# Reordering the gate/up steps of a two-layer Strassen kernel, and counting VectorE's 16-bit sums as held by GpSimd in its planner

## The chip, the cores and the metric

The kernel runs on one core of one Trainium2 chip. The metric is the device time of one execution in microseconds. The median of the kernel before is 1450.27 us over three runs (1448.57 to 1450.39).

## The reference, cut to what matters

Two kinds of block alternate, each added to its own input, on 2048 tokens of width 1024:

```python
def _A_ref(x, wqkv, wo):            # linear attention, 32 heads of 32
    q, k, v = heads(x @ wqkv)
    phi = lambda t: where(t > 0, t + 1, exp(t)) + 1e-6
    pq, pk = phi(q), phi(k)
    kv, z = einsum("bhsd,bhse->bhde", pk, v), einsum("bhsd->bhd", pk)
    o = einsum("bhqd,bhde->bhqe", pq, kv) / (einsum("bhqd,bhd->bhq", pq, z)[..., None] + 1e-6)
    return unheads(o) @ wo

def _B_ref(x, w_gate, w_up, w_down):   # F = 3584
    return ((x @ w_gate) * (x @ w_up)) @ w_down

x = x + _A_ref(_layernorm(x), A_wqkv, A_wo)
x = x + _B_ref(_layernorm(x), B_w_gate, B_w_up, B_w_down)
x = x + _A_ref(_layernorm(x), A_wqkv, A_wo)
x = x + _B_ref(_layernorm(x), B_w_gate, B_w_up, B_w_down)
```

Both A blocks use the same weights, and both B blocks too. So there are two layers, each an A block followed by a B block.

## The kernel before, in words

**Stages.** Each layer runs its A block as three stages: the key and query projections, the products that build the state ("g", with the normalization of the attention output), and the output projection ("y"). Then comes the B block in two halves of 1024 tokens. Each half is a gate/up stage followed by a down stage. There are so four gate/up stages, named here by layer and half: 1a, 1b, 2a, 2b. In the code their keys are `(False, 0)`, `(False, 1)`, `(True, 0)` and `(True, 1)`, where the first entry says "not the first layer" and the second is the half.

**A gate/up stage.** It has 14 *pairs* (`pair`, L1512). A pair is two *units* A and B, two blocks of 128 columns of w_gate (pairs 0, 2, 4 ...) or of w_up (pairs 1, 3, 5 ...). Each pair multiplies weights by activations with Strassen's seven products, numbered 1 to 7, instead of eight. Those products named in `L2SETS` (L357) use Strassen once more inside themselves: 5 in stage 1a; 5, 4 and 2 in stage 1b; 2, 5, 4 and 1 in the stages of layer 2. A plain product of one unit is four matmuls of 512 columns (L1539). A second-level product is done for both units at once by fourteen matmuls of 256 columns (L1657).

**Steps.** The order of a pair's work is a list of tokens written out by hand in `ORDERS` (L358). `gateup` (L1719) walks through that list once for each pair p and emits the instructions of each token, and every engine runs its own instructions in that order. A token with a prime (') does the step for pair p-1, one with a plus does it for p+1, so pairs overlap. At the end of the stage the primed tokens are emitted once more for the last pair (the *tail*), after the first matmuls of the down stage. The tokens are:

- `P1A`, `P6B` ...: the plain product of that number for unit A or B. TensorE does four matmuls, ScalarE copies the result to SBUF where a later step needs it (L1544), or into another PSUM bank (L1574).
- `51`, `55`, `56`, `57` (and `2n`, `4n`, `1n`): the steps of second-level product 5 (2, 4, 1). Each is two matmuls of 256 columns. Steps n1, n5 and n7 end in ScalarE copies (L1661, L1673); steps n6 and n7 end in a VectorE sum into PSUM (L1664), called a *seed* here.
- `D5A` and so on: the last products of a number into its result bank. For a second-level number A is four matmuls of 256 columns and B two.
- `F2A` and so on: the eviction. VectorE takes the result out of PSUM (L920). In an even pair the value is stored. In an odd pair it must also be multiplied into the value of the pair before (gate times up): VectorE writes one of three buffers (`utmp`) and GpSimd multiplies (L1563). In stage 1a evictions 1 and 4, which add nothing, are done by ScalarE in even pairs and by VectorE alone in odd ones.
- `S24`, `S5`, `S1`: the weight sums for the second level. In layer 1 they are four VectorE sums of 512 elements (`S24`) or of 256 elements (`S5`, `S1`) in 16 bits (all through the helper at L917), stored to DRAM for later; in layer 2, and `S5` in stage 1b, they are a DMA load instead.
- `T0`, `T1`: other work in small pieces (layer norm, saving the residual). In stage 1a they also make the first-level sums of a later unit (`prep_s`, L982: four VectorE sums of 512 elements, from the raw weights of that unit), store them to DRAM, and do the sums for the down weights (`wd_prep`).
- `R`: two loads of unit weights into a ring of five slots (`ring_issue`, L873). In iteration p it loads units 2p+3 and 2p+4 (counted from 0; pair p has units 2p and 2p+1). Every DMA of the kernel goes through the queue of SyncE in order of emission.
- `HA`, `HB`: nothing but, in stage 2a, four loads of the residual after the last pair.

**The planner.** Three kinds of section are not in the order of emission but in one found by a list scheduler (`reorder`, L155): the key/query stage of layer 2 (tag "kq2"), and the g and y stages of layer 1 (tags "g1" and "y1"). It gives each instruction a cost (`_cost`, L46 to L93) and a due time, makes twelve passes (`_pass`, L206) and keeps the order in which TensorE waits least by these costs. The last of the four values that `_cost` returns says whether the instruction needs the SBUF port that VectorE and GpSimd are taken to share: `_pass` starts such an instruction only when the one before it of that kind, on either engine, has ended (`gate`, L246).

Of the kernel before, what the change touches and what calls it, by code (L numbers as in the profile page):

```python
# [49 lines left out]
def _cost(op):  # L50
    seen = _Seen()
    op.fn(seen)
    name, args, kw = seen.calls[0]
    aps = [a for a in list(args) + list(kw.values()) if hasattr(a, "shape") and hasattr(a, "tensor")]

    def free(a):
        return int(np.prod(a.shape[1:]))

    def half(a):
        return a.dtype in (BF16, mybir.dt.float16)  # L60
    n = max(free(a) for a in aps)
    psum = any(a.tensor.name == "ps" for a in aps)
    packed = all(half(a) for a in aps if free(a) > 1)
    k = len(seen.calls)
    if op.eng == "sp":
        size = float(np.prod(aps[0].shape)) * (2 if half(aps[0]) else 4)
        if "transpose" in name:
            return 1240, 1240, size / 200, False
        return 70, 70, size / 300, False
    if op.eng == "pe":  # L70
        cols = free(args[0]) if name == "matmul" else 128
        one = max(cols / 2.4 + 2.5, 25)
        return k * one, (k - 1) * one + cols / 2.4 + 166, 0, False
    if op.eng == "act":
        c = 0.87 * n + 75
        return c, c + 104, 0, False
    if op.eng == "pool":
        c = 0.8 * n + 60 if name == "memset" else (580 if name == "tensor_tensor" else 304) if n < 64 else \
            (2.2 if packed else 2.45) * n if name == "tensor_tensor" else 1.15 * n + 20
        return c, c + 45, 0, n >= 64 and name != "memset"  # L80
    if name in ("bn_stats", "bn_aggr"):
        c = 635 if name == "bn_stats" else 126
    elif name == "tensor_reduce":
        c = 1150
    elif n < 64:
        c = 130 if name != "reciprocal" or n < 16 else 270
    elif name == "tensor_tensor":
        c = n / 1.92 + 68 if packed and not psum else n / 0.96 + 70
    elif name == "tensor_scalar" and not psum:
        c = n / (3.84 if packed else 1.92) + (140 if n > 512 else 70)  # L90
    else:
        c = n / 0.96 + 70
    return c, c + 84, 0, n >= 64 and not psum and name in ("tensor_scalar", "tensor_copy")  # L93


class _Prog:
# [58 lines left out]
    def reorder(self, tags):  # L155
# [6 lines left out]
        for e in _ENGS:  # L162
# [6 lines left out]
            for (_, ga), (_, gb) in zip(runs, runs[1:]):  # L169
                for x in gb:  # L170
                    preds[x].update(ga)
        occ, lat, load, port = zip(*(_cost(o) for o in ops))
        succ = [[] for _ in range(n)]
        for i in range(n):
# [160 lines left out]
def build_kernel(nc, A_x, A_wqkv, A_wo, B_w_gate, B_w_up, B_w_down, out):  # L335
# [20 lines left out]

    L2SETS = {(False, 0): "5", (False, 1): "542", (True, 0): "2541", (True, 1): "2541"}  # L357
    ORDERS = {  # L358
# [4 lines left out]
    }  # L363
    MUL_ENG = "pool"
# [125 lines left out]
    with ExitStack() as es:  # L490
# [13 lines left out]
        def vh(o, n):  # L504
            return ah[:, o // 2: o // 2 + n]
# [17 lines left out]
        T1, T2, T4 = [vh(O_T + i * 4096, 2048).rearrange("p (k s) -> p k s", s=512) for i in range(3)]  # L523
# [1749 lines left out]
def bass_interleave_layers__linear_attn_block__glu_gated_bilinear__prompt_kernel(  # L2273
    nc, A_x, A_wqkv, A_wo, B_x, B_w_gate, B_w_up, B_w_down, out,
):
    build_kernel(nc, A_x, A_wqkv, A_wo, B_w_gate, B_w_up, B_w_down, out)
# [28 lines left out]
```

## Time and profile before

| what | value |
|---|---|
| median of three runs | 1450.27 us |
| the profiled execution: its own time | 1451.07 us |
| the profiled execution: span on the core | 1449.3 us |
| granted TensorE clock | 1.00 |
| TensorE busy | 1426.1 us, 98% |
| VectorE busy | 1211.0 us, 84% |
| ScalarE busy | 618.9 us, 43% |
| GpSimd busy | 440.8 us, 30% |

The stages lie one after another in the span: gate/up 1a from about 240 to 411 us, 1b from 494 to 674 us, 2a from 970 to 1130 us and 2b from 1209 to 1369 us, with the down stages behind each. The key/query stage of layer 2 is at 748 to 846 us.

How to read it: in the views by window a row gives the length of the stretch, then for each engine its busy time and, in brackets, how many instructions lie in it, then the granted clock, the busy share of the DMA engines and the rate. In a timeline a row is the start, the time taken, the engine, the line, the operation, what it writes and reads, and how many neighbours were merged into the row; in square brackets stands the idle time before it and what ended it. Neighbours on VectorE overlap by some 0.1 us at their ends, so four sums in one row take less than four times one. Busy times of TensorE have modelled ends.

### The profile page before, as it was taken

To read this page: it belongs to the slowest core of one execution; us is meant where nothing else is said; L and a number is where in the kernel's file an instruction comes from. 1 tells how busy PE (TensorE), PEld (TensorE's weight loads), DVE (VectorE), ACT (ScalarE), POOL (GpSimd) and SP (SyncE) were. 2 spreads that over 40 slices of the span, in tenths; PEclk is the share of its full clock that TensorE was granted. 3 is DMA by queue.
4 is the path that set the end of the run, shared out by engine and by line. 5 is a ranking of instruction groups with operands and counts; after the bars stand their busy time and mean duration, and the time that the engine had idled before them with its cause. 6 is when DMAs were issued, how large, how long until landed. Compare 5 with 4: busy or idle time off the path is not lost.

```text
span 1449.3 us, 22852 instructions
## 1 busy us (share of the span) xinstructions
PE 1426.1 (98%) x8362; PEld 800.9 (55%) x8417; DVE 1211.0 (84%) x2282; ACT 618.9 (43%) x1292; POOL 440.8 (30%) x436
## 2 busy tenths in 40 slices
PE   9999999999999999999999999999999999999999
PEld 4444444454444555556574444456666677666557
DVE  8988898998968799998899869787877897777697
ACT  4332365444410255542037732566666114666402
POOL 4544631121210034342014447213443201342400
DMA  7446776999899889988782667688998769999667
GB/s 239 102 106 182 163 167 176 285 309 301 286 303 330 282 272 284 282 268 269 272 300 68 187 189 149 166 223 269 287 294 273 269 228 317 298 293 296 232 204 235
DMA packets 367040, 349.91 MB, mean 241 GB/s; under 512 B 107472, under 2 KB 308688, under 8 KB 366928
## 3 DMA queue, kind: packets, MB, share of 16 engines
q1 hardware_dynamic: 366928, 348.45, 79.5%
q8 instruction: 67, 1.10, 0.3%
q14 instruction: 45, 0.37, 0.1%
HBM read 255.72 MB, written 71.57 MB: 226 GB/s over the span
## 4 chain that ended last, share of the span: by engine, by line
PE 87%; DVE 7%; DMA 3%; issue 1%; ACT 1%; SPq 0%; POOL 0%; DVEq 0%; ACTq 0%
PE ps L1539 23%; PE ps L1657 16%; PE ps L1980 13%; PE ps L1097 8%; PE ps L2061 8%; PE ps L1440 8%; PE ps L1332 7%; PE ps L1161 3%; DVE arena L917 3%; DVE arena L920 2%; DMA arena<-in_B_w_gate_dram 1%; DVE ps L1664 1%; DMA arena<-in_A_wqkv_dram 1%; DMA arena<-xn_scratch 1%; PE ps L1355 0%
## 5 line engine op out<-in xcount | busy, mean ns | idle before, releaser
L1539 PE MATMUL ps<-arena 128*128 128x512 f16 x1824 | 453.2, 379 | 4.9 <-DVE arena L920 4.0
L920 DVE SCALAR_TENSOR_TENSOR arena<-ps,arena 128x512 f16<-128x512 f32 (+2 forms) x562 | 372.2, 683 | 70.7 <-PE ps L1980 29.7
L1563 POOL TENSOR_TENSOR arena<-arena 128x512 f16<-128x512 f16 x196 | 225.2, 1170 | 581.5 <-DVE arena L920 579.1
L917 DVE TENSOR_TENSOR arena<-arena 128x512 f16<-128x512 bf16 (+7 forms) x648 | 342.4, 569 | 15.3 <-PE ps L2061 4.9
L1657 PE MATMUL ps<-arena 128*128 128x256 f16 x2296 | 311.9, 273 | 6.3 <-DVE ps L1664 5.6
L1544 ACT ACTIVATE arena<-ps 128x512 f32<-128x512 f32 x308 | 184.3, 598 | 241.9 <-PE ps L1539 186.5
L1657 PEld LDWEIGHTS ps<-arena 128*128 128x128 f16 (+1 forms) x2296 | 214.8, 98 | 123.8 <-DVE ps L1664 27.5
L1539 PEld LDWEIGHTS ps<-arena 128*128 128x128 f16 (+1 forms) x1824 | 175.5, 98 | 150.9 <-DVE arena L920 9.8
L1664 DVE TENSOR_TENSOR ps<-ps,arena 128x256 f32<-128x256 f32 x328 | 141.2, 431 | 81.6 <-ACT ps L1661 34.7
L1980 PE MATMUL ps<-arena 128*128 128x512 f16 (+1 forms) x885 | 194.2, 379 | 1.0 <-POOL arena L1563 0.4
L1661 ACT COPY ps<-ps 128x256 f32<-128x256 f32 x328 | 109.9, 361 | 110.3 <-PE ps L1657 83.5
L1980 PEld LDWEIGHTS ps<-arena 128*128 128x128 f16 x896 | 87.3, 98 | 104.9 <-POOL arena L1563 0.9
L2061 PE MATMUL ps<-arena 128*128 128x256 f16 (+1 forms) x1176 | 129.8, 273 | 0.2
L1097 PE MATMUL ps<-arena 128*128 128x512 bf16 x563 | 125.8, 379 | 1.3 <-DMA arena<-in_A_wqkv_dram 0.5
L2061 PEld LDWEIGHTS ps<-arena 128*128 128x128 f16 x1176 | 114.7, 98 | 15.6 <-ACT ps L2067 1.0
L1332 PE MATMUL ps<-arena 128*128 128x512 bf16 x499 | 114.9, 379 | 2.0 <-DMA arena<-xn_scratch 1.0
L1440 PE MATMUL ps<-arena 128*128 128x512 bf16 x502 | 110.3, 379 | 0.5
L1226 POOL TENSOR_TENSOR arena<-arena 128x1024 f16<-128x1024 f32 x32 | 80.8, 2525 | 85.5 <-DVE arena L1224 82.8
L1120 POOL TENSOR_TENSOR arena<-arena 128x512 f32<-128x512 f32 x60 | 72.6, 1216 | 80.0 <-DVE arena L811 40.7
L1097 PEld LDWEIGHTS ps<-arena 128*128 128x128 f16 x576 | 55.8, 98 | 67.0 <-DMA arena<-in_A_wqkv_dram 1.4
L618 DVE BATCH_NORM_STATS2 arena<-arena 128x6 f32<-128x512 bf16 x128 | 87.8, 688 | 5.6 <-DMA arena<-in_A_x_dram 3.7
L1161 PE MATMUL ps<-arena 128*128 128x512 f16 (+1 forms) x385 | 85.4, 379 | 1.5 <-DVE arena L831 0.6
(69 smaller groups left out, 950.6 us busy)
## 6 DMA issues: line engine op xcount, KB each, us to landing
arena<-s_scratch SPq DMA_DIRECT2D x84, 512.0 KB, 6.3
arena<-d_images SPq DMA_DIRECT2D x36, 896.0 KB, 5.3
arena<-in_B_w_gate_dram SPq DMA_DIRECT2D x56, 512.0 KB, 5.9
arena<-in_B_w_up_dram SPq DMA_DIRECT2D x56, 512.0 KB, 5.5
arena<-t_scratch SPq DMA_DIRECT2D x20, 896.0 KB, 4.9
arena<-p_scratch SPq DMA_DIRECT2D x66, 256.0 KB, 4.6
s_scratch<-arena SPq DMA_DIRECT2D x28, 512.0 KB, 6.4
arena<-p_scratch SPq DMA_DIRECT2D x28, 512.0 KB, 5.7
```

Source lines behind the costliest of these rows:

```text
L917: P.add("dve", lambda e: e.tensor_tensor(out=out, in0=a, in1=b, op=op), rd=rd, wr=wr, prd=prd)
L920: P.add("dve", lambda e: e.scalar_tensor_tensor(out=out, in0=a, scalar=sc, in1=b, op0=ALU.mult, op1=op1), rd=rd, wr=wr, prd=prd)
L1097: P.add("pe", lambda e: [e.matmul(psb(bank), xnT[:, k, i * 128:(i + 1) * 128], w[:, k, h * 512:(h + 1) * 512], start=(k == 0), stop=(k == ...
L1332: return [e.matmul(psb(bank), xr[:, t, j * 128:(j + 1) * 128], pk[:, h, t, :], start=(start and t == ts[0]), stop=(stop and t == ts[-1]), ...
L1440: return [e.matmul(psb(bank), xnT[:, g, i * 128:(i + 1) * 128], wp[:, g, dh * 512:(dh + 1) * 512], start=(dh == 0 and g == 0), stop=(g == ...
L1539: P.add("pe", lambda e: [e.matmul(psb(bank), w[:, k, :], x[:, k, :], start=(start and k == 0), stop=(k == 3), skip_group_check=True) for k ...
L1544: P.add("act", lambda e: e.activation(t, psb(bank), AF.Copy, scale=SG), prd=[bank], wr=r)
L1563: P.add(MUL_ENG, lambda e: e.tensor_tensor(out=hx, in0=ut, in1=hx, op=ALU.mult), rd=ur + hr, wr=hr)
L1657: P.add("pe", lambda e: [e.matmul(psb(bank)[:, 256 * half:256 * half + 256], w[:, k, :], xx[:, k, :], start=(start and k == 0), stop=(k == ...
L1664: P.add("dve", lambda e: e.tensor_tensor(out=psb(bank)[:, 256:512], in0=psb(src)[:, 0:256], in1=c5, op=ALU.add), prd=[src], rd=rc5, pwr=[b ...
L1980: P.add("pe", lambda e: [e.matmul(psb(bank), hv[:, 7 * hf + k, t * 128:(t + 1) * 128], w[:, k, :], start=(q in fresh and hf == 0 and k == ...
L2061: P.add("pe", lambda e: [e.matmul(half(b, h), x[:, k, :], w[:, k, :], start=(bool(start) and k == 0), stop=(k == 6), skip_group_check=True ...
```

## The change

Two things are changed. First, in `_cost` VectorE's `tensor_tensor` on operands that are all 16 bits wide and lie in SBUF now counts as needing the shared port, as `tensor_scalar` and `tensor_copy` did already. Its assumed duration is the same. This is used by the planner alone, so it acts on the order in "kq2", "g1" and "y1". Second, three of the four token lists are replaced (1a, 1b and 2a); that of 2b stays.

```diff
-    return c, c + 84, 0, n >= 64 and not psum and name in ("tensor_scalar", "tensor_copy")
+    return c, c + 84, 0, n >= 64 and not psum and (name in ("tensor_scalar", "tensor_copy") or packed and name == "tensor_tensor")
...
     ORDERS = {
-        (False, 0): "51' P7A' 55' P6B' F1A' T0' 56' HA' D4A' F4A' HB' T1' P7B' D2B' 57' P1A D5A' F2A' D4B' D2A S5 D5B' F2B' D3A' F4B' F3A' F1B' P6A D3B' F3B' R P1B",
-        (False, 1): "P7A' D2B' F1B' HA 57' 41' D5A' 45' F2A' P7B' 46' P1A S5 D5B' S24 D3A' T0' F2B' 47' D4A' F4A' S1' 21 25 P1B D3B' D4B' 26 F3A' R P6A F4B' F3B' HB 27 51 P6B D2A 55 F1A 56 T1'",
-        (True, 0): "P7A' 41' HB' D5A' HA' F2A' 57' P7B' D2B' 45' F1B' 46' D5B' F2B' D3A' S24 47' S1+ 11 D4A' 15 16 D3B' F4A' 17 21 P1A F3A' D4B' 25 26 P1B F4B' P6A F3B' 51 27 P6B D2A S5 F1A 55 56 T0 R T1",
+        (False, 0): "56' P7A' P6B' HB' D5A' D4A' T0' F2A' F4A' 57' P7B' D2B' F1B' T1' P1A D5B' D4B' D2A F2B' F4B' R D3A' F3A' P6A HA' 51 S5 F1A P1B D3B' 55 F3B'",
+        (False, 1): "D2B' F1B' 55' 56' T1' P7A' 57' 41' P7B' 45' S1' 46' D5A' D5B' S5 S24 F2A' F2B' P1A HA 47' D4A' F4A' P1B 25 21 D3A' F3A' P6A T0 D4B' 51 26 HB F4B' D3B' F3B' 27 D2A P6B F1A R",
+        (True, 0): "D2A' 55' F1A' HA' HB' 56' T1' P7A' 41' D5A' F2A' 57' P7B' D2B' 45' F1B' S1+ 46' D5B' F2B' D3A' 47' 11 D4A' 15 16 F4A' D3B' 17 S5 21 P1A 25 F3A' S24+ D4B' 26 F4B' T0 R F3B' P1B P6A 51 27 P6B",
```

Every list holds the same tokens as before apart from their primes and pluses, so the number of instructions of each kind in a stage is the same; only their order on the engines and in SyncE's queue changes.

## The prediction

> **What bounds the kernel now.** I read the page's head first, then the stages by windows (columns as explained above).
>
> ```profile
> PE 1426.1 (98%) x8362; PEld 800.9 (55%) x8417; DVE 1211.0 (84%) x2282; ACT 618.9 (43%) x1292; POOL 440.8 (30%) x436
> ```
> ```profile
> 113.80:183.60 69.80, 69.38 (x371) 33.70 (x378) 58.39 (x82) 19.69 (x33) 36.52 (x15) 1.00 0.72 185
> 183.60:239.50 55.90, 55.64 (x256) 25.25 (x258) 51.13 (x115) 32.68 (x45) 17.17 (x30) 1.00 0.73 175
> 239.50:410.90 171.40, 168.52 (x874) 84.65 (x873) 147.59 (x339) 78.08 (x155) 32.22 (x30) 1.00 0.92 280
> ...
> 494.00:674.30 180.30, 171.50 (x1063) 99.38 (x1063) 162.96 (x339) 88.02 (x210) 69.64 (x72) 1.00 0.88 272
> ...
> 747.90:846.30 98.40, 95.45 (x431) 42.12 (x438) 88.61 (x183) 70.66 (x117) 43.39 (x48) 1.00 0.58 176
> ...
> 969.70:1130.40 160.70, 160.60 (x1108) 104.58 (x1109) 121.66 (x234) 100.58 (x246) 61.63 (x57) 1.00 0.84 264
> ...
> 1208.90:1368.60 159.70, 159.59 (x1105) 104.42 (x1105) 114.81 (x221) 99.65 (x245) 58.43 (x53) 1.00 0.91 281
> ```
>
> TensorE is the bound, and its idle time lies in few places: 8.80 us in stage 1b (180.30 - 171.50), 2.88 in 1a, 2.95 in the key/query stage, 0.10 in 2a, 0.42 and 0.26 in g and y of layer 1. Only these can be won. Stage 1b has fewer matmuls than 2a (1063 against 1108) and takes 19.6 us longer, with VectorE busy for 162.96 us of it. The chain that ended last gives the pace:
>
> ```profile
> 505.82 1.73 PE ps L1539 x8
> ...
> 656.58 1.73 PE ps L1539 x8
> ...
> 850.18 3.45 PE ps L1332 x16
> ...
> 991.76 1.81 PE ps L1657 x16
> ...
> 1117.30 1.82 PE ps L1657 x16
> ```
>
> In 1b the same piece returns every two pairs, six times in 150.76 us: 25.13 us for two. In 2a a piece returns every pair, eleven times in 125.54 us: 11.41. A matmul of 512 columns takes 3.45/16 = 0.216 us, one of 256 takes 1.81/16 = 0.113. A pair of 1b has 32 and 42 of them, one of 2a 24 and 56, so on TensorE alone 1b would need 11.41 + 8 x 0.216 - 14 x 0.113 = 11.56 us a pair, 23.12 for two. Lost are 2.0 us in every two pairs, **14 us** in the stage's seven.
>
> Where they go, a timeline shows. The same sums stand in it twice, four of 256 and four of 512 elements, in two successive iterations:
>
> ```profile
> 581.24 1.01 DVE L917 TENSOR_TENSOR arena<-arena 128x256 f16<-128x256 bf16 x4
> ...
> 583.29 1.88 DVE L920 SCALAR_TENSOR_TENSOR arena<-ps,arena 128x512 f16<-128x512 f32 x3
> ...
> 589.73 2.52 POOL L1563 TENSOR_TENSOR arena<-arena 128x512 f16<-128x512 f16 x2 [1.26 <-DVE arena L920]
> ...
> 590.83 2.51 DVE L917 TENSOR_TENSOR arena<-arena 128x512 f16<-128x512 bf16 x4
> ...
> 594.58 1.04 PE L1539 MATMUL ps<-arena 128*128 128x512 f16 x4 [0.95 <-DVE arena L920]
> 594.61 2.32 POOL L1563 TENSOR_TENSOR arena<-arena 128x512 f16<-128x512 f16 x2 [2.35 <-DVE arena L920]
> ...
> 595.37 2.23 DVE L917 TENSOR_TENSOR arena<-arena 128x256 f16<-128x256 bf16 x4
> ...
> 598.00 0.61 PE L1657 MATMUL ps<-arena 128*128 128x256 f16 x4 [0.79 <-DVE ps L1664]
> ...
> 598.23 0.63 SPq L589 DMA_DIRECT2D arena<-in_B_w_up_dram  x1
> ...
> 604.17 1.55 DVE L917 TENSOR_TENSOR arena<-arena 128x512 f16<-128x512 bf16 x4
> ```
>
> Where GpSimd multiplies, `S24` takes 2.51 instead of 1.55 us and `S1'` 2.23 instead of 1.01; TensorE then waits on VectorE (0.95, 0.79). The excess is 0.96 + 1.22 = 2.18 us in one iteration of two, 15.3 in seven: the size of the loss. Without it VectorE has 162.96 - 15.3 = 147.7 us, 10.5 a pair against TensorE's 11.56.
>
> **Part 1, the list of 1b.** It moves the sums away from the multiplies, if my placing by hand is right. Two durations for it, from the page's groups:
>
> ```profile
> L1664 DVE TENSOR_TENSOR ps<-ps,arena 128x256 f32<-128x256 f32 x328 | 141.2, 431 | 81.6 <-ACT ps L1661 34.7
> ...
> L618 DVE BATCH_NORM_STATS2 arena<-arena 128x6 f32<-128x512 bf16 x128 | 87.8, 688 | 5.6 <-DMA arena<-in_A_x_dram 3.7
> ```
>
> TensorE's positions in the new list (0.216 and 0.113 a matmul, from the start of an iteration): D2B' ends at 0.2, 57' 1.7, 46' 3.2, D5B' 3.9, D4A' 5.4, D3A' 7.6, D4B' 8.7, 26 9.1, D3B' 9.9, 27 10.2, D2A 10.6, the end at 11.6. VectorE's order is F1B' 56' T1' 57' S1' 46' S24 F2A' F2B' 47' F4A' F3A' T0 26 F4B' F3B' 27 F1A. An eviction takes 0.63 in a row of three (1.88/3), a seed 0.34 (0.43 less the 0.1 by which neighbours overlap), a T some 0.7, one `bn_stats`. F1B' runs from 0.4, S1' from 2.7 to 3.7, S24 from 4.0 to 5.6, F2A' and F2B' to 6.9, F4A' to 7.8, F3A' to 8.4, T0 to 9.1, F4B' and F3B' to 10.8, the seed of 27 to 11.2, F1A to 11.8. VectorE keeps up, by some 0.3 us.
>
> Multiplies exist for odd pairs, so in one iteration of two. F1A's runs to about 1.6 of the next iteration and F1B's to 2.8 (2.52/2 = 1.26 each); the other six begin at 6.2, when both sums are over. They run seven to eight us and end near 2 in the iteration after, ahead of S1' again. So S24 is free and S1' touches the end of one multiply. In the old order F1B' and F2A' came before S24, and F2B' and F4A' before S1'. From both sides: all 14 us won, or none. I take a remainder of 0.35 us in each of seven iterations, between the 0.1 us of overlap that I place and the 0.96 that a whole S24 pays now: 14 - 2.5 = **-11.5 us**.
>
> `R` moves to the end, and its weights are needed by the next iteration's S24 at 4.0, so by 15.6. SyncE reaches it behind S24's store (5.6) and, where T0 stores a norm, behind that (9.1). That leaves 6.5 to 10 us. Before, loads issued at 598.23 fed S24 at 604.17, 5.9 us later, without a wait in that row. I cost it at nothing.
>
> **Part 2, the list of 1a.** Two stalls stand out, one view for the wait and one for the load; the third fence is the page's:
>
> ```profile
> 284.19 2.35 DVE L917 TENSOR_TENSOR arena<-arena 128x512 f16<-128x512 bf16 x6 [1.39 <-DMA arena<-in_B_w_gate_dram]
> ...
> 357.45 2.35 DVE L917 TENSOR_TENSOR arena<-arena 128x512 f16<-128x512 bf16 x6 [2.10 <-DMA arena<-in_B_w_gate_dram]
> ```
> ```profile
> 276.38 7.79 DMA arena<-in_B_w_gate_dram
> ...
> 349.15 8.28 DMA arena<-in_B_w_gate_dram
> ```
> ```profile
> arena<-in_B_w_gate_dram SPq DMA_DIRECT2D x56, 512.0 KB, 5.9
> ```
>
> The load waits in SyncE's queue behind the store of S5's sums. In the new list R stands ahead of S5, after D4B' at 7.2, and T1' needs the data after D2B' at 5.2 rather than before it: two to three us more lead, above the 2.10 that was missing. Won: up to 3.5 us (1.39 + 2.10). Against it, T0' now runs ahead of F4A', and T1' ahead of F4B'. With 2.35 us for its six sums and 0.7 for a norm, F4A' of an odd pair ends near 5.0 where P1A wants its bank at 5.2, and F4B' near 9.9 where P1B wants its bank at 10.0. A miss of up to 0.7 in each of seven iterations costs 5 us; I take 2. S5's sums now fall beside F3A's multiply, where VectorE has the lighter next iteration to catch up. Sum **-1.5 us**, bounds -3.5 and +5.
>
> **Part 3, the list of 2a.** Cyclically TensorE's order is the old one but for D4B' and 25 changing places; the list begins elsewhere, so the tail is longer and the first iteration shorter. Its sums are loads, S24 a pair earlier and S5 later. TensorE idles 0.10 us here: **0**, bounds -0.1 and +1, about one step's chain of copies at the start.
>
> **Part 4, the planner.** Neither engine's work changes. In the key/query stage 2.95 us are idle; I take **-0.5**, bounds -3 and +3 (as much again). g and y have 0.7 idle together: 0, to +2, one misplaced product of L1226 (row below).
>
> The rule that speaks against this part is told beside its rows:
>
> ```profile
> L1226 POOL TENSOR_TENSOR arena<-arena 128x1024 f16<-128x1024 f32 x32 | 80.8, 2525 | 85.5 <-DVE arena L1224 82.8 <-DVE arena L640 2.7
> ...
> L1217 DVE TENSOR_TENSOR arena<-arena 128x1024 f32<-128x1024 bf16 x20 | 23.5, 1182 | 0.1
> ...
> L1214 DVE SCALAR_TENSOR_TENSOR arena<-arena 128x1024 f32<-128x1024 bf16 x12 | 16.8, 1401 | 0.0
> ```
>
> The Trainium skill (SBUF — State Buffer, "Who interferes with whom") lets any VectorE instruction with two SBUF inputs contend with a GpSimd instruction that reads SBUF, whatever its width. By that rule the norm's products L1217 and L1214 would be held too while the planner still counts them free; the means here do not show a hold, and the sum by the rule would take the +2 of g and y.
>
> **Sum.** -11.5 - 1.5 + 0 - 0.5 = -13.5 us, made against the profiled execution: 1451.07 (span 1449.3) to 1437.6. The median lies 0.8 lower, 1450.27, so **1436.8 us**.
>
> **The rivals.** *Half of it (1444).* VectorE keeps up in 1b by 0.3 us only, and D2B' needs the seed of 27, which stands behind F4B' and F3B'. An extra piece of norm in T (0.7) or a held S1' then makes TensorE wait 0.4 to 0.7 in most iterations: 14 x 0.5 = 7 back, -6.5. For it: VectorE's 10.5 of 11.56. Against: iterations without multiplies keep up now with the same work.
>
> *The holds stay (1448).* The multiplies follow the evictions wherever these go; if GpSimd runs a multiply or two later than I place it, S1' and S24 fall under it as now, and only the 2.0 of the other parts is won. Against: six of eight evictions now stand behind S24.
>
> *Late weights in 1b (1459, slower).* If SyncE comes to R only in its place, after F1A and D2A at 10.6, S24 has 5.0 us where a load takes 5.9 in the median and 7.79 or 8.28 at worst. VectorE would stand still there and everything queued behind S24 with it, F2A' first, then TensorE. VectorE's slack is 1.06 a pair, so the loss is 13 x (wait - 1.06): with 7.79 it is 13 x (2.79 - 1.06) = 22, less the 13.5 of the sum, so 9 us slower than before. It decides above a wait of 2.1 us, where 13 x 1.04 eats the 13.5. For it: the DMA share of 1b rises from 0.88 to some 0.94 as the stage shortens. Against: the lead above, and 2b, at 0.91 with R last in its list, idles 0.11 us.
>
> *The planner's stages lose (1442):* the bounds above, +5, taken with the rest won.
>
> **Chances.** Forecast 0.55 (its own range 1433 to 1441), half 0.20, planner 0.06, holds stay 0.09, late weights 0.10. About 0.2% (2.9 us) is what a measurement can tell from no change. Faster by more: 0.55 + 0.20 + 0.06, same 0.09, slower 0.10. The range is 1431 to 1448: below, all of 14 + 3.5 + 3 less 1; above, the half (-6.5) with 1a at +2.5 in place of -1.5, some 4 us more.
>
> **What would show it.** Part 1: in 1b's groups the 256- and 512-element sums of L917 fall from means of 489 and 563 ns to about 290 and 420, and two pairs take 23 to 23.5 us. The group rows for that:
>
> ```profile
> L917 DVE TENSOR_TENSOR arena<-arena 128x512 f16<-128x512 bf16 x39 | 20.9, 563 | 0.4
> L917 DVE TENSOR_TENSOR arena<-arena 128x256 f16<-128x256 bf16 x42 | 19.4, 489 | 0.5
> ```
>
> Part 2: no wait for w_gate above 1 us in 1a; against it, waits of L1539 on L920 there. Part 3: 2a within 1 us of 160.7. Part 4: TensorE's idle time in 748 to 846. Wrong would be a gap on VectorE ahead of S24 put down to w_gate or w_up (late weights), or idle TensorE ahead of D2B' put down to L1664 (half).

## The result, and the profile after

The changed kernel takes 1438.74 us (median of four runs, 1438.32 to 1439.24) against 1450.33 us beside it. The ratio is 0.9919, with a 95% interval of 0.9902 to 0.9936: 0.8% faster, 9 to 14 us. The forecast was 1436.8 us, with a range of 1431 to 1448.

The page of the changed kernel, its head and the first groups:

```profile
span 1436.9 us, 22892 instructions
PE 1427.0 (99%) x8417; PEld 804.0 (56%) x8417; DVE 1196.4 (83%) x2282; ACT 618.8 (43%) x1292; POOL 438.7 (31%) x436
...
PE 94%; DVE 2%; ACT 1%; DMA 1%; issue 0%; SPq 0%; POOL 0%; DVEq 0%; ACTq 0%
...
L1539 PE MATMUL ps<-arena 128*128 128x512 f16 x1824 | 449.5, 379 | 0.7 <-ACT ps L1574 0.7
```

The last two of these rows, on the page of the kernel before:

```profile
PE 87%; DVE 7%; DMA 3%; issue 1%; ACT 1%; SPq 0%; POOL 0%; DVEq 0%; ACTq 0%
...
L1539 PE MATMUL ps<-arena 128*128 128x512 f16 x1824 | 453.2, 379 | 4.9 <-DVE arena L920 4.0
```

The span is 12.4 us shorter (1449.3 to 1436.9). VectorE does the same 2282 instructions in 14.6 us less (1211.0 to 1196.4), and of the chain that ended last 94% is now TensorE's instead of 87%. TensorE's wait ahead of L1539 fell from 4.9 to 0.7 us. By stages (from the start of the first matmul to the start of the last one for a gate/up stage; for the others from there to the first matmul of the next):

| stage | before, us | after, us | difference |
|---|---|---|---|
| gate/up 1a | 171.9 | 168.6 | -3.3 |
| gate/up 1b | 175.2 | 167.6 | -7.7 |
| the down stage behind 1b | 78.8 | 78.1 | -0.7 |
| key/query of layer 2 | 93.3 | 92.9 | -0.4 |
| gate/up 2a | 161.4 | 161.0 | -0.3 |
| gate/up 2b (list not changed) | 161.0 | 161.9 | +0.9 |
| all others | 607.7 | 606.8 | -0.9 |

Of the 0.9 of 2b, 0.7 is a wait of TensorE for a load from `p_scratch` at its start. The stage ran from 161.0 to 162.8 us in the kernels below, all with the same 2b list, so it is not counted as an effect of the change.

Stage 1b by window, in the changed kernel:

```profile
490.00:658.00 168.00, 165.99 (x1046) 100.01 (x1045) 148.99 (x338) 86.79 (x210) 65.10 (x69) 1.00 0.96 291
```

In 1b VectorE is busy for 148.99 us instead of 162.96, and TensorE is idle for 2.01 us (168.00 - 165.99) instead of 8.80. The groups of its sums in that window, and the wait that stayed:

```profile
L917 DVE TENSOR_TENSOR arena<-arena 128x512 f16<-128x512 bf16 x40 | 15.7, 419 | 0.5
...
L917 DVE TENSOR_TENSOR arena<-arena 128x256 f16<-128x256 bf16 x42 | 10.8, 285 | 0.5
L655 DVE TENSOR_SCALAR arena<-arena 128x1024 f16<-128x1024 bf16 x8 | 6.2, 775 | 2.0 <-POOL arena L634 2.0
```

The means fell from 563 and 489 ns to 419 and 285. The timeline of 1b shows where the multiplies went, and one iteration that is still late:

```profile
537.25 6.72 POOL L1563 TENSOR_TENSOR arena<-arena 128x512 f16<-128x512 f16 x6 [3.97 <-DVE arena L920]
...
545.63 0.55 DVE L655 TENSOR_SCALAR arena<-arena 128x1024 f16<-128x1024 bf16 x1 [1.00 <-POOL arena L634]
546.09 0.43 DVE L1664 TENSOR_TENSOR ps<-ps,arena 128x256 f32<-128x256 f32 x1
...
546.42 1.01 DVE L917 TENSOR_TENSOR arena<-arena 128x256 f16<-128x256 bf16 x4
...
546.57 0.39 PE L1657 MATMUL ps<-arena 128*128 128x256 f16 x2 [0.37 <-DVE ps L1664]
```

Six multiplies run in one block from 537.25 to 543.97, after both sums of their iteration; the next S1' at 546.42 takes 1.01 us, unheld. Ahead of it VectorE stood still for 1.00 us until GpSimd had finished a small chain for a norm (L634), so the seed at 546.09 came late and TensorE waited 0.37. The pace of 1b in the chain of the changed kernel:

```profile
525.96 1.73 PE ps L1539 x8
537.60 1.73 PE ps L1539 x8
549.96 1.82 PE ps L1539 x8
561.70 1.73 PE ps L1539 x8
574.06 1.83 PE ps L1539 x8
```

An iteration takes 11.64 us (537.60 - 525.96) where nothing waits, and 12.36 where the norm is late (549.96 - 537.60 and 574.06 - 561.70). Two iterations are 23.28 us without such a wait (2 x 11.64) and 24.10 with one (561.70 - 537.60). Before, two iterations took 25.13.

### The profile page after: what moved, and what is told of

Same layout as the page of the kernel before. It is cut to its first block, busy times and chain, and to the rows that moved or that the text cites. A ratio compares the mean times of both kernels' runs of the same rounds, so it can differ in the third digit from the quotient of the medians.

```text
span 1436.9 us, 22892 instructions
## 1 busy us (share of the span) xinstructions
PE 1427.0 (99%) x8417; PEld 804.0 (56%) x8417; DVE 1196.4 (83%) x2282; ACT 618.8 (43%) x1292; POOL 438.7 (31%) x436
## 4 chain that ended last, share of the span: by engine, by line
PE 94%; DVE 2%; ACT 1%; DMA 1%; issue 0%; SPq 0%; POOL 0%; DVEq 0%; ACTq 0%
PE ps L1539 27%; PE ps L1657 17%; PE ps L1980 13%; PE ps L1097 9%; PE ps L1440 8%; PE ps L2061 8%; PE ps L1332 7%; PE ps L1161 4%; DVE arena L920 1%; DMA arena<-xn_scratch 1%; PE ps L1355 1%; PE ps L1383 0%; DMA arena<-p_scratch 0%; ACT arena L652 0%; DVE arena L618 0%
## 5 line engine op out<-in xcount | busy, mean ns | idle before, releaser
L1539 PE MATMUL ps<-arena 128*128 128x512 f16 x1824 | 449.5, 379 | 0.7 <-ACT ps L1574 0.7
L1563 POOL TENSOR_TENSOR arena<-arena 128x512 f16<-128x512 f16 x196 | 223.8, 1163 | 477.4 <-DVE arena L920 475.0
L917 DVE TENSOR_TENSOR arena<-arena 128x512 f16<-128x512 bf16 (+7 forms) x648 | 326.7, 544 | 12.1 <-PE ps L2061 4.9
L1657 PE MATMUL ps<-arena 128*128 128x256 f16 x2296 | 308.2, 273 | 2.7 <-DVE ps L1664 2.0
L1539 PEld LDWEIGHTS ps<-arena 128*128 128x128 f16 (+1 forms) x1824 | 176.4, 98 | 146.3 <-ACT ps L1574 1.2
L1980 PE MATMUL ps<-arena 128*128 128x512 f16 (+1 forms) x896 | 195.2, 379 | 0.0
L1226 POOL TENSOR_TENSOR arena<-arena 128x1024 f16<-128x1024 f32 x32 | 80.5, 2515 | 85.6 <-DVE arena L1224 81.4
L1161 PE MATMUL ps<-arena 128*128 128x512 bf16 (+1 forms) x392 | 85.6, 379 | 0.8 <-ACT ps L1182 0.8
```

The lines of the kernel that those rows point to most:

```text
L917: P.add("dve", lambda e: e.tensor_tensor(out=out, in0=a, in1=b, op=op), rd=rd, wr=wr, prd=prd)
L1161: P.add("pe", lambda e: [e.matmul(psb(bank), l[:, k, :], w[:, k, :], start=(start and k == 0), stop=(k == 3), skip_group_check=True) for k ...
L1539: P.add("pe", lambda e: [e.matmul(psb(bank), w[:, k, :], x[:, k, :], start=(start and k == 0), stop=(k == 3), skip_group_check=True) for k ...
L1563: P.add(MUL_ENG, lambda e: e.tensor_tensor(out=hx, in0=ut, in1=hx, op=ALU.mult), rd=ur + hr, wr=hr)
L1657: P.add("pe", lambda e: [e.matmul(psb(bank)[:, 256 * half:256 * half + 256], w[:, k, :], xx[:, k, :], start=(start and k == 0), stop=(k == ...
L1980: P.add("pe", lambda e: [e.matmul(psb(bank), hv[:, 7 * hf + k, t * 128:(t + 1) * 128], w[:, k, :], start=(q in fresh and hf == 0 and k == ...
```

## The experiments

### Each part by itself

Four kernels carry one edit each: the planner's line, or one of the three lists as the change has it.

```diff
# e1_cost: the kernel before, and
+    return c, c + 84, 0, n >= 64 and not psum and (name in ("tensor_scalar", "tensor_copy") or packed and name == "tensor_tensor")
# e2_1b: the kernel before, with the new list of (False, 1)
# e3_1a: the kernel before, with the new list of (False, 0)
# e4_2a: the kernel before, with the new list of (True, 0)
```

> The kernel before with the planner's cost line alone (16-bit VectorE sums counted as needing the shared port); the four token lists stay old. Theory: the stages that the planner orders idle little, so this part is worth -0.5 us or less (1449.8), with the key/query stage of layer 2 some 0.3 us shorter. Rival, the planner carries a good share of the gain (the sums of the key/query stage are no longer held): -2 to -4 us. Other rival, it loses: +1 to +3.

> The kernel before with the new token list of stage 1b alone. Theory: this list is the larger part; -7.7 us in the stage and -0.7 in the down stage behind it (TensorE no longer waits for a multiply there), so 1442. Rival, 1b gains only together with 1a (its first weights and residuals come from 1a's queue order): -4 or less.

> The kernel before with the new token list of stage 1a alone. Theory: the two waits for w_gate go, -3.3 us (1447.0), and nothing else moves. Rival, what 1a wins is lost again in the down stage behind it or in 1b: within 1 us of before.

> The kernel before with the new token list of stage 2a alone. Theory: TensorE idled 0.1 us in this stage, so nothing to win: within 0.7 us of 1450.3. Rival, the longer tail and later loads cost: +1 to +2.

| kernel | ratio to before, 95% interval | its own stage, us |
|---|---|---|
| planner's line | 0.9994 (0.9985 to 1.0003) | key/query 93.3 to 92.8 |
| list of 1b | 0.9945 (0.9933 to 0.9958) | 1b 175.2 to 167.2, down stage behind it 78.8 to 78.1 |
| list of 1a | 0.9974 (0.9965 to 0.9983) | 1a 171.9 to 168.7 |
| list of 2a | 0.9999 (0.9990 to 1.0008) | 2a 161.4 to 161.1 |

The parts add up: the four ratios multiply to 0.9912, and all together measured 0.9919. Two thirds of the gain is 1b, nearly all the rest 1a. For the planner's line and for 2a no effect can be told from none in the time. Of the two kinds of edit in the change it is the lists that pay.

### Are the holds the cause in 1b?

The 56 multiplies of stage 1b are left out, in the old and in the new order.

```diff
-                        P.add(MUL_ENG, lambda e: e.tensor_tensor(out=hx, in0=ut, in1=hx, op=ALU.mult), rd=ur + hr, wr=hr)
+                        if not (first and ps_):
+                            P.add(MUL_ENG, lambda e: e.tensor_tensor(out=hx, in0=ut, in1=hx, op=ALU.mult), rd=ur + hr, wr=hr)
```

> The kernel before, with GpSimd's 56 multiplies of stage 1b left out (gate times up isn't formed there, so the second half of layer 1's block B is not the reference's). The evictions of VectorE stay. Theory, the holds by the multiplies make stage 1b slow: without them, in the old order, S24 takes 1.55 and S1' 1.01 us in every iteration and the stage falls from 175.2 to 163 to 167 us; time 1438 to 1442. Rival, the old order itself (which eviction stands ahead of which seed) makes it slow: the stage stays above 172 us and the time above 1447.

> The changed kernel, with the same 56 multiplies of stage 1b left out. Theory, the new order has hardly any holds left, and what remains over TensorE's own time in 1b (some 4.7 us) is the wait of a norm for its own statistics and the stage's start: less than 1.5 us to be won, 1437.3 to 1438.7. Rival, holds of S1' by F1A's and F1B's multiplies make the rest: 3 to 4 us to be won, 1435.

The old order without multiplies: 1441.18 us, ratio 0.9928 (0.9914 to 0.9943), stage 1b 165.3 us instead of 175.2. The new order without them: 1438.59, stage 1b 167.1 instead of 167.6. So the multiplies cost the old order 10.0 us in this stage and cost the new one 0.5. The groups of the sums in 1b, in the old order without multiplies:

```profile
L917 DVE TENSOR_TENSOR arena<-arena 128x512 f16<-128x512 bf16 x40 | 15.7, 420 | 1.6 <-DMA arena<-in_B_w_up_dram 1.0
L917 DVE TENSOR_TENSOR arena<-arena 128x256 f16<-128x256 bf16 x42 | 10.9, 286 | 0.5
```

They match the changed kernel's 419 and 285 to a nanosecond: the new order reaches with the multiplies what the old one reaches only without them. The multiplies could also have cost time by keeping a `utmp` buffer from VectorE, but in stage 1b of the kernel before no wait of VectorE is put down to them; what they lengthen is the sums themselves. And without any multiplies the old order is the better one by 1.8 us (165.3 against 167.1): the new list pays something for its arrangement.

### One step put back under the multiplies

```diff
-... 46' D5A' D5B' S5 S24 F2A' F2B' P1A HA ...
+... 46' D5A' D5B' S5 F2A' F2B' S24 P1A HA ...
```

> The changed kernel with one step moved: S24 of stage 1b behind F2A' and F2B' instead of ahead of them, so that its four sums fall under their multiplies in odd-even iterations. Theory of holds: S24 takes some 2.5 to 3.5 us instead of 1.55 in seven iterations; VectorE is ahead by only 0.3 us, so most of it reaches TensorE: +5 to +9 us, 1444 to 1448. Rival, VectorE catches up within the two iterations: +0 to +2 us.

Measured: 1446.73 us, ratio to before 0.9971 (0.9961 to 0.9981); stage 1b 175.1 us, 7.6 more than in the changed kernel and as long as before the change. One move of one token gives the whole gain of 1b back. Its timeline:

```profile
537.92 2.45 POOL L1563 TENSOR_TENSOR arena<-arena 128x512 f16<-128x512 f16 x2 [2.51 <-DVE arena L920]
538.35 3.09 DVE L917 TENSOR_TENSOR arena<-arena 128x512 f16<-128x512 bf16 x4
539.50 0.60 PE L1657 MATMUL ps<-arena 128*128 128x256 f16 x4 [0.21 <-DVE arena L917]
```

S24 takes 3.09 us instead of 1.55 under two multiplies, and stands as the last releaser of a TensorE wait. By 543.1 TensorE is 1.15 us further behind the changed kernel than it was ahead of this S24. Behind the next S24 (552.17), which stands at the same place of the list with no multiply beside it and takes 1.55 us, it falls no further behind. So the loss comes from the hold and not from the place as such.

### What is left in 1b: the norm's pieces

The string says how many pieces of norm each T of stage 1b runs. Where a T has two, a tile's statistics and its normalization can stand back to back, with GpSimd's chain between them. First each T got one piece; then two pieces alone were moved one T later.

```diff
-                    for _ in range(int("1111111012010211121101111111"[u])):
# e9_flat
+                    for _ in range(int("1111111111111111111111111111"[u])):
# e11_pieces
+                    for _ in range(int("1111111011110121121101111111"[u])):
```

> The changed kernel with the norm pieces of stage 1b dealt out one to each T, where the list of counts now puts two into some and none into others. Theory: two pieces in one T put a normalization directly behind its own statistics, VectorE waits 1.00 us for GpSimd's small chain, and the seed behind it is late for TensorE; without that the two such iterations lose 0.5 to 0.7 us less each: -1 to -2 us, 1437. Rival, the pieces only move the lateness to other iterations: within 0.7 us of 1438.7.

> The changed kernel with two pieces of norm in stage 1b each moved one T later (in the iterations where one T holds the statistics of a tile and, right behind them, its own normalization); no piece comes earlier than now, so no transpose does either. Theory: the two waits of 1.00 us of VectorE for GpSimd's small chain go, and with them two waits of TensorE of 0.53 us and what follows: stage 1b -1 to -1.5 us, time 1437.2 to 1437.9, against 1438.7. Rival, the lateness only moves to the next T: stage 1b within 0.5 us.

One piece to each T was a miss: 1442.45 us, stage 1b 170.7 us, 3.1 slower than the changed kernel. The norm's transposes come earlier by it, and they became a new wait:

```profile
618.86 1.02 DVE L917 TENSOR_TENSOR arena<-arena 128x256 f16<-128x256 bf16 x4 [3.00 <-DMA arena<-arena]
...
620.28 1.02 PE L1657 MATMUL ps<-arena 128*128 128x256 f16 x6 [2.60 <-DVE ps L1664]
```

S1' keeps its sums in columns that a transpose has still to finish filling; it waits 3.00 us for that, and TensorE 2.60 behind it. The kernel before and the changed one share these columns too: by their order of emission, sums of S1' stand in the upper four of the eight row blocks of the first three token tiles when layer 2's key and query products read them. So in both kernels layer 2's keys and queries of these 384 tokens are in part computed from weight sums in place of the normalized input, which the reference does not do. Both do it alike, so the comparison of times is not touched. With the two pieces moved later, so that no transpose comes earlier, the theory held, by a little more than was expected: 1437.04 us, ratio 0.9902 (0.9889 to 0.9916), stage 1b 166.0 us, 1.6 less than in the changed kernel. Both waits of L655 for L634 are gone from the trace. The two ratios' intervals overlap, so that this kernel beats the changed one is shown by the stage, not by the total.

### What stopped the waits for weights in 1a

In the changed kernel R of 1a goes back behind S5; in the kernel before it goes ahead of S5.

```diff
# e7_r_late, the changed kernel
-... D2A F2B' F4B' R D3A' F3A' P6A HA' 51 S5 F1A P1B D3B' 55 F3B'
+... D2A F2B' F4B' D3A' F3A' P6A HA' 51 S5 R F1A P1B D3B' 55 F3B'
# e8_r_early, the kernel before
-... F2A' D4B' D2A S5 D5B' F2B' ... D3B' F3B' R P1B
+... F2A' D4B' D2A R S5 D5B' F2B' ... D3B' F3B' P1B
# e12_r_order, the kernel before
+... F2A' D4B' D2A D5B' R S5 F2B' ... D3B' F3B' P1B
```

> The changed kernel with the two weight loads of stage 1a (R) put back behind S5 in the token list, so that they queue behind the store of S5's sums. Theory of the prediction, R ahead of S5 removes the waits for w_gate: they come back, 2 to 3 us slower (1441). Rival, the wait went because T1' comes later in the new list: within 0.7 us of 1438.7.

> The kernel before with R of stage 1a put ahead of S5 (behind D2A), all else old. Theory of the prediction: loads go out 1 to 2 us sooner, the waits of 1.39 and 2.10 us for w_gate shrink or go: -2 to -3 us (1447.5 to 1448). Rival, the place of T1' decides: within 0.7 us of before.

> The kernel before with D5B', R and S5 of stage 1a in this order, where S5 stood first and R at the end: no compute engine's own order changes, only SyncE's, in which the two weight loads now stand ahead of the store of S5's sums. Theory of the prediction (a load waits behind that store): the waits of 1.39 and 2.10 us for w_gate go, stage 1a -2 to -3.3 us, 1447 to 1448.5. Rival (where T1' needs the weights decides): stage within 0.7 us of 171.9.

With R back behind S5 the changed kernel's 1a is 0.4 us longer (169.0), and 1439.83 us in all: the waits for w_gate and w_up are 0.4 and 0.3 us. So in the new list the place of R hardly matters. What else the list changes is enough, and of that the later T1' is what bears on these loads; no run moves T1' alone.

The second kernel told nothing on the question. It took 1468.56 us, ratio 1.0115 (1.0098 to 1.0132). Near the end of 1a R loads weights of the down stage, and these fill more of a slot than raw gate/up weights do. D5B' reads sums in that slot, and here it stood behind R:

```profile
390.36 0.60 PE L1657 MATMUL ps<-arena 128*128 128x256 f16 x2 [6.82 <-DMA arena<-t_scratch]
...
413.09 0.61 PE L1657 MATMUL ps<-arena 128*128 128x256 f16 x2 [8.37 <-DMA arena<-in_B_w_down_dram]
```

It waited 6.82 and 8.37 us for those loads, 15.2 of the 18.9 us that stage 1a grew by (and it then took the loaded weights for the sums that they had overwritten, so a part of 1a is not the reference's in this kernel). The third kernel has D5B' ahead of R and changes the order of SyncE alone. It took 1448.98 us, ratio 0.9983 (0.9975 to 0.9992), with 1a at 170.2 us, 1.7 less than before. One wait for w_gate of 1.6 us is left of 3.5. So the loads did wait behind the store of S5's sums, and going ahead of it is worth half of what 1a won; the rest of the new list, without it, is worth nearly all of it (169.0 us).

## Why the prediction was right, point by point

**The time.** Forecast -13.5 from 1450.27, so 1436.8; measured -11.6, 1438.74. The likeliest case came, within its own range (1433 to 1441), with two terms off in opposite directions (1b by 3.1 us, 1a by 1.8). That the total is closer than 1b's term is luck in part.

**Part 1, 1b: -11.5 forecast, -8.4 measured** (7.7 in the stage, 0.7 in the down stage behind it, where TensorE no longer waits 0.4 us for a multiply at the tail: not forecast; that down stage took 78.5 to 78.8 us with the old list of 1b and its multiplies, so some of the 0.7 is chance). The mechanism was right at each step that the trace can show: S24 is free, S1' too, VectorE's busy time fell by 14.0 where 15.3 was worked out, and the multiplies run in one block of 6.72 us where seven to eight were placed.

Mis-sized was the term "14 us won, all or none". It is 2.0 us times seven, but the loss occurs six times in the stage: the multiplies of the last odd pair run in the tail, and by the starts of the stage's matmuls six iterations of the kernel before took over 13 us (13.04 to 14.07). The unheld pace was right: most iterations of the old order without multiplies take 11.54 us, where 11.56 was worked out. So the loss was 150.76 - 12 x 11.54 = 12.3 us, and it was put down to the holds as a whole because 15.3 us of excess on VectorE was of the same size. Taking the multiplies away shows 10.0 in the stage. The other 2.3 have nothing to do with holds: without multiplies three iterations of the old order are still long (12.84, 12.02 and 12.00 us). The remainder set for S1' (2.5) was too large instead: 0.5 is what the multiplies still cost the new order.

The reading that 1b takes 19.6 us longer than 2a was too large as well, since its window holds some 5 us of the down stage; from first to last matmul it is 13.9 (175.2 - 161.4).

**The half rival** had a true core. Its mechanism, an extra piece of norm that makes a seed late because VectorE is ahead by little, is what the changed kernel still loses: 1.6 us with two pieces moved. It expected that in most iterations; it was in two, because most T have one piece.

**Late weights in 1b** did not come, though the DMA share rose to 0.96 (0.94 was expected). No wait of VectorE for w_gate or w_up stands in 1b, so the loads came in time. In one iteration the first load of R, which the next S24 needs, was issued at 549.62 and that S24 starts at 559.13: 9.5 us ahead, where 6.5 to 10 was worked out. The rival **the holds stay** fell by the means of 419 and 285 ns.

**Part 2, 1a: -1.5 forecast, -3.3 measured** (-3.2 alone). The gain side, 3.5, came nearly whole. The cost side, 2 us for P1A and P1B waiting on evictions behind a T, did not come at all: the only wait of TensorE's matmuls listed in 1a is 0.7 at its start, for ScalarE, and VectorE's waits for w_gate are gone. The step that failed is the placing of F4A' and F4B' at 0.1 to 0.2 us from where they would be late; it was done with six sums and a piece of norm in every T, but only four `bn_stats` stand in the whole stage. In the iteration of an odd pair that starts near 302.3, F4A' is over at 306.81 and P1A starts near 307.45. The reason given for the gain was half right: R ahead of S5 gains 1.7 in the old order, but in the new one 0.4, most likely because T1' wants the data later.

**Part 3, 2a: 0 forecast**, -0.3 in the trace and nothing in the time.

**Part 4, the planner: -0.5 forecast**, 0.9994 (0.9985 to 1.0003), 0.5 less in the key/query stage. Over all the traces here that stage takes 93.2 to 93.5 us with the old line and 92.8 to 93.1 with the new one, so the stage shows the gain though the time does not. The prediction took the means of the norm's products as a sign that nothing holds them. Single rows of the kernel before say otherwise:

```profile
861.68 1.91 POOL L1226 TENSOR_TENSOR arena<-arena 128x1024 f16<-128x1024 f32 x1 [0.54 <-DVE arena L1224]
...
861.76 2.90 DVE L1214 SCALAR_TENSOR_TENSOR arena<-arena 128x1024 f32<-128x1024 bf16 x1
...
866.44 1.16 DVE L1214 SCALAR_TENSOR_TENSOR arena<-arena 128x1024 f32<-128x1024 bf16 x1
866.61 2.76 POOL L1226 TENSOR_TENSOR arena<-arena 128x1024 f16<-128x1024 f32 x1 [3.02 <-DVE arena L1224]
```

Where GpSimd's product (L1226) starts first it takes 1.91 us, and VectorE's behind it 2.90. Where VectorE's starts first it takes 1.16, and GpSimd's behind it 2.76. So these products do hold each other, and mostly it is GpSimd that pays: 23 of the 32 L1226 took 2.76 us. The rule of the Trainium skill (SBUF — State Buffer, "Who interferes with whom") by which the norm's products would be held too agrees with these rows. That it would add the 2 us of g and y no run here shows: with the planner's line alone neither stage of layer 1 changed (69.8 and 55.3 us).

## What to carry to other kernels

When one engine's sums are slow in every second iteration only, look for what another engine does in those iterations alone, and compare the same instruction with and without it in one timeline: that gives the price of a hold without any run. Look at single executions and not at a mean, which mixes held and free ones. Then count how often the loss really occurs, and size the gain by taking the suspected cause out, not by the distance to the best pace, since a part of that distance can be other waits. A token list that places work to the tenth of a microsecond is easily spoiled: one token moved cost 7.6 us here, and evening out the small pieces brought a transpose forward into a buffer that was still in use.

## What the runs showed of the hardware that was not expected

The hold is a plain wait and leaves no trace once the two no longer meet: 128x512 and 128x256 sums take 419 and 285 ns in the changed kernel and 420 and 286 with the multiplies gone, against means of 563 and 489 before. Such a mean hides two kinds: of the 42 sums of 512 elements in 1b before, 35 took 411 to 426 ns and seven 639 to 1380. GpSimd's own multiply stayed at 1170 and 1163 ns. So in stage 1b the price is paid nearly whole by VectorE, whose held sums mostly started second, and seven tenths of it reached the end time (10.0 us in the stage, of the 14.0 by which VectorE's busy time fell). In the norm it is GpSimd's product that mostly starts second, and there GpSimd pays (2.76 us instead of 1.91).
